# Queries of the first two token tiles from raw x with a ones column, and their normalised tiles transposed by DMA

## The chip, the cores and the metric

One core of one Trainium2 chip. The metric is the device time of one execution in microseconds; lower is better. Medians over several executions are quoted with their range. A ratio is the mean time of one kernel's fast runs over the mean of the other's fast runs of the same rounds, so it is not quite the ratio of the two medians.

A profile is one execution.

## The reference

Two layers, each made of a sliding local attention (32 heads of 32, 8 positions back at a distance of 2) and a dense block of 1024 to 3584 with GELU. Cut to what matters:

```python
x = A_x                                        # [1, 2048, 1024] bf16
for layer in range(2):
    n = layernorm(x)                           # no gain, no bias
    q, k, v = split(n @ wqkv)                  # [1024, 3072]
    logits = sum(q[s] * k[s - 2*w] for each of 8 w) * 32**-0.5
    x = x + (softmax(logits) * v windows) @ wo
    x = x + (gelu(layernorm(x) @ w1 + b1) @ w2 + b2)
```

## The kernel before

Tokens are worked in four groups of 512, each of four tiles of 128 tokens. The order for group 0 is: queries of tiles 0 and 1 (the weights arrive meanwhile), queries of tiles 2 and 3, then K and V of all four tiles, then queries and K of group 1 while VectorE does group 0's attention, and at about 123 us the output projection of group 0, which reads the attention output `oT`. All loads go out from one engine (SP) in program order, in one queue. Normalised tiles of group 1 and 2 reach their transposed form by transposing DMAs in that same queue.

The start, which the change replaces:

```python
load_x(0, 0, 2)                                 # tiles 0, 1
for k in range(0, KD, 2):                       # query weights in four pieces of 512 KB
    load_wq_piece(wq_first[k // 4], k)
    if k < 4: load_x(0, 2 + k // 2, 3 + k // 2)
...
warm_up(14)                                     # dummy matmuls, no result used
stats(0); stats(1)                              # VectorE, root on ScalarE
xn0 = norm(0); xn1 = norm(1, (0, 2 * P, D))
transpose_on_pe(xn0, ...); transpose_on_pe(xn1, ...)
stats(2); stats(3)
...
# then the queries of tiles 0 and 1 from the normalised, transposed tiles
```

```python
wk = load_qkv(1)                                # 2 x 1 MB
load_x(2)                                       # tiles 8 to 11
early_tiles = ln_early((1, None), (2, qk_next))
for _ in range(NTT): next(early_tiles)          # tiles 4..7: statistics, norm, DMA transpose
wv = load_qkv(2)                                # V weights, 2 x 1 MB, BEHIND the transposes
for _ in early_tiles: pass                      # tiles 8, 9
```

## Time and profile before

| | before |
|---|---|
| median of the first three runs | 1230.72 us (1230.47 to 1231.24) |
| first useful matmul | 8.26 us |
| K of group 0 starts on PE | 23.19 us |
| VectorE's first attention product | 26.82 us |
| second half of the V weights issued, landed | 27.09, 35.92 us |
| the same needed by PE | 37.86 us |
| last attention output of group 0 ready, needed | 123.92, 124.85 us |
| span of the profile | 1228.4 us |

The other shows itself as a place with nothing in it; this is PE's timeline around the start of V in the kernel before (start, length, instruction):

```profile
35.71 5.56 PE L117 MATMUL acc<-xnT,wt 128*128 128x512 bf16 x25
```

Twenty-five matmuls in one run, no bracket: the V weights were 37.86 - 35.92 = 1.94 us early, and no view of waits shows a margin. It has to be looked up from the landing of the transfer.

### The profile page before, as it was taken

Reading aid. Unit: us, or ns where it says so; the run is one execution under the profiler, and the core shown is the slowest. Engines: PE = TensorE matmul, PEld = TensorE weight load, DVE = VectorE, ACT = ScalarE, POOL = GpSimd, SP = SyncE. Lnnn points to the kernel's source line nnn. Section 1 sums busy time; section 2 is a strip of 40 time slices with the busy share of each in tenths; the row PEclk is TensorE's granted clock in tenths of the full one; section 3 lists DMA queues with packets and bytes.
Section 4 is the critical chain, followed back from the end, with each engine's and each line's share of the span. In section 5 each row is a group of like instructions: output and inputs, shape, how many; then the busy total and the mean of one; then the engine's idle time right before and its main releaser. Section 6 shows DMA issues by size and latency. Waiting matters only on the chain.

```text
span 1228.4 us, 13955 instructions
## 1 busy us (share of the span) xinstructions
PE 1221.6 (99%) x5720; PEld 632.7 (52%) x5770; DVE 861.5 (70%) x912; ACT 315.6 (26%) x497; POOL 120.9 (10%) x219
## 2 busy tenths in 40 slices
PE   9999999999999999999999999999999999999998
PEld 7666544456444564446544465444654444444444
DVE  7999896998898999375993759937599797011001
ACT  5343253014310233202431024410244001300310
POOL 2330025010101101100001000000000002000000
PEclk9999999999999999999999999999999999999999
DMA  9965674766638645856557565576664558446441
GB/s 302 290 206 164 176 233 151 202 178 199 219 128 245 188 150 166 239 170 175 161 158 230 172 171 181 157 216 201 171 200 147 186 194 209 149 159 194 156 135 52
DMA packets 223647, 226.64 MB, mean 185 GB/s; under 512 B 71824, under 2 KB 190752, under 8 KB 221536
## 3 DMA queue, kind: packets, MB, share of 16 engines
q1 hardware_dynamic: 214704, 208.69, 56.3%
q0 software_dynamic: 8880, 17.07, 4.2%
q8 instruction: 45, 0.74, 0.2%
q14 instruction: 18, 0.15, 0.0%
HBM read 189.01 MB, written 4.19 MB: 157 GB/s over the span
## 4 chain that ended last, share of the span: by engine, by line
PE 99%; DVE 0%; issue 0%; DMA 0%
PE acc L117 99%; DMA x<-in_A_x_dram 0%; DVE stats L92 0%; PE acc L211 0%; DVE xn L92 0%; DVE x L92 0%; DVE mv L92 0%; DVE rstd L92 0%
## 5 line engine op out<-in xcount | busy, mean ns | idle before, releaser
L117 PE MATMUL acc<-xnT,wt 128*128 128x512 bf16 (+1 forms) x3392 | 720.3, 375 | 0.1
L117 PEld LDWEIGHTS <-wt 128*128 128x128 bf16 x3392 | 400.8, 120 | 317.4
L117 PE MATMUL acc<-wt,hT 128*128 128x512 bf16 (+1 forms) x1780 | 386.0, 376 | 2.1
L117 PEld LDWEIGHTS <-hT 128*128 128x128 bf16 x1820 | 178.1, 98 | 209.0
L92 DVE TENSOR_TENSOR big<-big 128x1024 bf16<-128x1024 bf16 (+2 forms) x184 | 244.8, 1359 | 2.2
L92 ACT ACTIVATE hT<-acc,b1T 128x512 bf16<-128x512 f32 x224 | 152.1, 687 | 325.9 <-PE acc L117 325.8
L92 DVE TENSOR_TENSOR big<-qT,kT 128x4096 bf16<-128x4096 bf16 x64 | 143.8, 2283 | 36.3 <-ACT kT L92 35.9
L92 DVE TENSOR_TENSOR big<-abc,vT 128x4096 bf16<-128x4096 bf16 x64 | 144.6, 2284 | 11.0 <-DMA abc<-a 7.1
L92 DVE TENSOR_TENSOR tmp<-acc,b2bc 128x512 f32<-128x512 f32 x56 | 38.6, 689 | 159.8 <-PE acc L117 156.7
L92 ACT CAST qT<-acc 128x512 bf16<-128x512 f32 (+1 forms) x72 | 38.0, 543 | 276.8 <-PE acc L117 274.6
L117 PE MATMUL acc<-wt,oT 128*128 128x512 bf16 x440 | 97.6, 379 | 0.4
L92 DVE BATCH_NORM_STATS2 stats<-x 128x6 f32<-128x512 bf16 x116 | 77.4, 681 | 6.0 <-DMA x<-in_A_x_dram 5.0
L117 PEld LDWEIGHTS <-oT 128*128 128x128 bf16 x448 | 43.8, 98 | 53.0 <-issue 0.3
L92 DVE TENSOR_TENSOR x<-acc,big 128x512 bf16<-128x512 f32 (+1 forms) x9 | 5.7, 632 | 90.0 <-PE acc L117 90.0
L92 POOL TENSOR_TENSOR rstd<-mv,eps_t 128x1 f32<-128x1 f32 x54 | 16.7, 308 | 524.2 <-DVE mv L92 524.2
L92 ACT CAST vT<-acc 128x512 bf16<-128x512 f32 x64 | 37.4, 585 | 101.9 <-PE acc L117 101.9
L92 ACT CAST kT<-acc 128x512 bf16<-128x512 f32 x64 | 37.3, 584 | 64.5 <-PE acc L117 64.5
L92 DVE TENSOR_TENSOR x<-acc,x 128x512 bf16<-128x512 f32 x64 | 42.9, 670 | 5.1 <-PE acc L117 4.7
L92 DVE TENSOR_SCALAR xn<-x,mv,rstd 128x1024 bf16<-128x1024 bf16 (+2 forms) x53 | 28.5, 540 | 20.1 <-POOL rstd L92 19.9
L92 DVE TENSOR_TENSOR x<-tmp,x 128x512 bf16<-128x512 f32 x56 | 38.6, 689 | 1.4
L92 POOL DMA_DIRECT2D big<-big x24 | 13.3, 563 | 212.5 <-DVE big L92 212.5
L92 ACT ACT_TABLE_LOAD x17 | 21.8, 1283 | 38.9 <-DVE e L92 30.5
(62 smaller groups left out, 285.4 us busy)
## 6 DMA issues: line engine op xcount, KB each, us to landing
wt<-in_B_w_dram SPq DMA_DIRECT2D x56, 1024.0 KB, 5.6
wt<-in_B_w_dram SPq DMA_DIRECT2D x64, 896.0 KB, 4.8
wt<-in_A_wqkv_dram SPq DMA_DIRECT2D x46, 1024.0 KB, 5.6
wt<-in_A_wo_dram SPq DMA_DIRECT2D x16, 1024.0 KB, 5.0
abc<-a POOLq DMA_DIRECT2D x32, 256.0 KB, 4.6
big<-big POOLq DMA_DIRECT2D x24, 256.0 KB, 3.8
x<-in_A_x_dram SPq DMA_DIRECT2D x16, 256.0 KB, 7.1
out_dram<-x SPq DMA_DIRECT2D x31, 128.0 KB, 1.8
```

Source lines behind the costliest of these rows:

```text
L92: inst = f(*args, **kwargs)
L117: return pe(nc.tensor.matmul(*args, **kwargs))
```

## The change

The intent is to begin useful matmuls without waiting for VectorE's statistics. Layer normalisation is (x - mean) * rstd, so q = (x W - mean * sum(W)) * rstd. PE transposes the raw x of tiles 0 and 1, multiplies weights by it, and a column of ones beside the tokens (two are written, one is read) gives sum(W) in the same matmuls. Afterwards VectorE adds -mean * sum(W), and GpSimd multiplies by rstd. Mean and rstd lie by token on partitions and are needed along the free axis; four fp32 transposes on PE spread them. K and V still need the normalised tiles 0 and 1, which two DMA transposes now provide. The first loads are issued by two engines. Cut to its core:

```diff
-    load_x(0, 0, 2)
-    for k in range(0, KD, 2): load_wq_piece(...)         # 512 KB pieces, SP
+    SP:  x0, wq rows 0, 2, 3, x3, wq rows 5, 6, 7         # 256 KB pieces
+    ACT: x1, wq row 1, x2, wq row 4
...
-    warm_up(14)
-    stats(0); stats(1); norms; transposes of the normalised tiles
+    warm_up(8); transposes of raw x[0], x[1]; warm_up(4)
+    stats(0); root(0); stats(1); root(1)
+    less = -mean; rstd = 1 / root
+    norm(0), norm(1)                    -> first_early   (for K and V)
+    # after three of eight weight rows:
+    for column in (less0, less1, rstd0, rstd1):
+        pe(nc.tensor.transpose(bank[...], column.to_broadcast([P, P]), identf[:]))   # fp32
+    rest():  stats(2), root(2), norm(2), stats(3), root(3), norm(3)
...
+    def finish(c):
+        vec.scalar_tensor_tensor(out=part[:, c, :], in0=less, scalar=first[c][:, NT:NT + 1],
+                                 in1=first[c][:, 0:NT], op0=ALU.mult, op1=ALU.add)
+        pool.tensor_tensor(out=qT[:, c, 0:NT], in0=part[:, c, :], in1=rstd, op=ALU.mult)
+    for c in range(7): finish(c)        # ahead of the statistics of tile 4
...
-            wk = load_qkv(1)
+            for xn, out in first_early: sp.dma_start_transpose(out, xn...)
+            wk = load_qkv(1, lambda: load_x(1, 2, 3))     # tile 6 between the halves
+            load_x(1, 3, 4)                               # tile 7 behind them
...
-            ahead = ln_stats(tiles[i + 1][0])              # rstd by GpSimd
+            ahead = ln_stats(tiles[i + 1][0], root=True)   # root on ScalarE
+            vec.reciprocal(mv_rstd[1][:], mv_rstd[1][:])   # one more op on VectorE
```

More of the change, by code (lines that the diff above doesn't have):

```diff
@@ L119, with load_x, load_qkv @@
     x = [xpool.tile([P, D], BF16, name=f"x{t}") for t in range(S // P)]
-    def load_x(g, t0=0, t1=NTT):
+    def load_x(g, t0=0, t1=NTT, engine=None):
         for tt in range(t0, t1):
             t = g * NTT + tt
-            sp.dma_start(x[t][:], x_in[t * P:(t + 1) * P, :])
-    def load_qkv(which):
+            (engine or sp).dma_start(x[t][:], x_in[t * P:(t + 1) * P, :])
+    def load_qkv(which, between=None):
         tiles = []
@@ L130, in load_qkv, with load_wq_row @@
             sp.dma_start(wt[:], wqkv_v[:, h * (KD // 2):(h + 1) * (KD // 2), which * D:(which + 1) * D])
+            if h == 0 and between:
+                between()
             tiles.append(wt)
         return tiles
-    def load_wq_piece(wt, k):
-        sp.dma_start(wt[:, k % (KD // 2):k % (KD // 2) + 2, :], wqkv_v[:, k:k + 2, 0:D])
-    load_x(0, 0, 2)
+    def load_wq_row(k, engine):
+        engine.dma_start(wq_first[k // (KD // 2)][:, k % (KD // 2), :], wqkv_v[:, k, 0:D])
+    load_x(0, 0, 1)
     wq_first = [wpool.tile([P, KD // 2, D], BF16, name="wt") for _ in range(2)]
-    for k in range(0, KD, 2):
-        load_wq_piece(wq_first[k // (KD // 2)], k)
-        if k < 4:
-            load_x(0, 2 + k // 2, 3 + k // 2)
+    for k in (0, 2, 3):
+        load_wq_row(k, sp)
+    load_x(0, 3, 4)
+    for k in range(5, KD):
+        load_wq_row(k, sp)
     warm = bigp.tile([P, P], BF16, name="big")
@@ L150 @@
     one = const.tile([P, 1], F32, name="one")
+    act.on = True
     act.activation(one[:], eps_t[:], ACT.Sqrt)
+    load_x(0, 1, 2, act)
+    load_wq_row(1, act)
+    load_x(0, 2, 3, act)
+    load_wq_row(4, act)
+    act.on = False
     ident = const.tile([P, P], BF16, name="ident")
     make_identity(nc, ident[:])
+    identf = const.tile([P, P], F32, name="identf")
+    make_identity(nc, identf[:])
     mask = const.tile([P, W - 1, HALO], F32, name="mask")
@@ L174, in load_b2, with ln_stats @@
         pool.dma_start(b2bc[:], B_b2.unsqueeze(0).to_broadcast([P, D]))
-    def ln_stats(t, mv=None, rstd=None):
+    def ln_stats(t, mv=None, rstd=None, root=False):
         stats = lnp.tile([P, 2, 6], F32, name="stats")
@@ L183, in ln_stats @@
         vec.bn_aggr(mv[:], stats[:])
+        if root:
+            std = lnp.tile([P, 1], F32, name="std")
+            act.activation(std[:], mv[:, 1:2], ACT.Sqrt, bias=eps_t[:])
+            return mv, std
         pool.tensor_tensor(out=rstd[:], in0=mv[:, 1:2], in1=eps_t[:], op=ALU.add)
@@ L206, in ln_norm, with transpose_on_pe, copy_transposed @@
         return xn
-    def transpose_on_pe(xn, out, parts):
-        pst = psum.tile([P, KD, P], BF16, name="acc", bufs=8)
-        for k in range(parts[0][0], parts[-1][1]):
+    def transpose_on_pe(xn, out, bank, parts=(0, KD)):
+        pst = bank[:].bitcast(BF16).rearrange("p (k t) -> p k t", t=P)
+        for k in range(KD):
             pe(nc.tensor.transpose(pst[:, k, :], xn[:, k * P:(k + 1) * P], ident[:]))
-        for k0, k1, copy in parts:
-            copy(out[:, k0:k1, :], pst[:, k0:k1, :])
+        copy_transposed(out, bank, parts)
+    def copy_transposed(out, bank, parts):
+        pst = bank[:].bitcast(BF16).rearrange("p (k t) -> p k t", t=P)
+        for k0, k1 in zip(parts[:-1], parts[1:]):
+            act.copy(out[:, k0:k1, :], pst[:, k0:k1, :])
     last_transpose = [None]
@@ L220, in ln_tile @@
         last_transpose[0] = sp.dma_start_transpose(xnT[:, tt, :, :], xn[:].rearrange("s (k p) -> s k p", p=P))
-    first_late = []
+    first_early, first_late = [], []
+    NT = 2 * P
     def ln_first():
-        xa[0] = new_xnT()
+        xnT = xa[0] = new_xnT()
         vec.on = act.on = True
-        mvs = {}
-        stds = {}
+        raw = attp.tile([P, KD, NT + 2], BF16, name="vT", bufs=2)
+        vec.memset(raw[:, :, NT:NT + 2], 1.0)
+        mv = lnp.tile([P, 4, 2], F32, name="mvs", bufs=1)
+        std = lnp.tile([P, 4], F32, name="stds", bufs=1)
+        rstd = lnp.tile([P, 4], F32, name="rstds", bufs=1)
+        less = lnp.tile([P, 2], F32, name="lesses", bufs=1)
         def stats(tt):
@@ L234, in stats @@
                 vec.bn_stats(st6[:, h, :], x[tt][:, h * HALF:(h + 1) * HALF])
-            mvs[tt] = lnp.tile([P, 2], F32, name="mv")
-            vec.bn_aggr(mvs[tt][:], st6[:])
-            stds[tt] = lnp.tile([P, 1], F32, name="std")
-            act.activation(stds[tt][:], mvs[tt][:, 1:2], ACT.Sqrt, bias=eps_t[:])
-        def norm(tt, bounds=(0, D)):
-            rstd = lnp.tile([P, 1], F32, name="rstd")
-            vec.reciprocal(rstd[:], stds[tt][:])
-            xn = lnp.tile([P, D], BF16, name="xn", bufs=3)
-            for lo, hi in zip(bounds[:-1], bounds[1:]):
-                vec.tensor_scalar(out=xn[:, lo:hi], in0=x[tt][:, lo:hi], scalar1=mvs[tt][:, 0:1], scalar2=rstd[:],
-                                  op0=ALU.subtract, op1=ALU.mult)
-            return xn
+            vec.bn_aggr(mv[:, tt, :], st6[:])
@@ new lines, in root, with norm @@
+        def root(tt):
+            act.activation(std[:, tt:tt + 1], mv[:, tt, 1:2], ACT.Sqrt, bias=eps_t[:])
+        def norm(tt, out):
+            if tt > 1:
+                vec.reciprocal(rstd[:, tt:tt + 1], std[:, tt:tt + 1])
+            vec.tensor_scalar(out=out, in0=x[tt][:], scalar1=mv[:, tt, 0:1], scalar2=rstd[:, tt:tt + 1],
+                              op0=ALU.subtract, op1=ALU.mult)
+            return out
+        warm_ps = acc_tile()
+        warm_up(8, warm_ps)
+        banks = [acc_tile(), acc_tile()]
@@ L249, in ln_first @@
+        for tt in range(2):
+            transpose_on_pe(x[tt], raw[:, :, tt * P:(tt + 1) * P], banks[tt], (0, 2))
+        warm_up(4, warm_ps)
         stats(0)
+        root(0)
+        for tt in range(2):
+            copy_transposed(raw[:, :, tt * P:(tt + 1) * P], banks[tt], (2, KD))
         stats(1)
-        xn0 = norm(0)
-        xn1 = norm(1, (0, 2 * P, D))
-        transpose_on_pe(xn0, xa[0][:, 0, :, :], [(0, 2, act.copy), (2, 8, act.copy)])
-        transpose_on_pe(xn1, xa[0][:, 1, :, :], [(0, 2, vec.tensor_copy)])
@@ L255, in ln_first, with spread_stats @@
-        transpose_on_pe(xn1, xa[0][:, 1, :, :], [(2, 8, act.copy)])
-        stats(2)
-        stats(3)
-        for tt in range(2, 4):
-            first_late.append((norm(tt), xa[0][:, tt, :, :]))
-        vec.on = act.on = False
-        act.hold()
+        root(1)
+        vec.tensor_scalar(out=less[:], in0=mv[:, 0:2, 0], scalar1=-1.0, scalar2=None, op0=ALU.mult)
+        vec.reciprocal(rstd[:, 0:2], std[:, 0:2])
+        by_token = iop.tile([P, 4, P], F32, name="tmp")
+        def spread_stats(bank):
+            for i, column in enumerate((less[:, 0:1], less[:, 1:2], rstd[:, 0:1], rstd[:, 1:2])):
+                pe(nc.tensor.transpose(bank[:, i * P:(i + 1) * P], column.to_broadcast([P, P]), identf[:]))
+            rows = by_token[:].rearrange("p i t -> p (i t)")
+            act.copy(rows, bank[:])
+            return rows[:, 0:NT], rows[:, NT:2 * NT]
@@ new lines, in ln_first, with rest, queries_of_raw, row @@
+        xn = bigp.tile([P, 2, D], BF16, name="big")
+        first_early.append((norm(0, xn[:, 0, :]), xnT[:, 0, :, :]))
+        first_early.append((norm(1, xn[:, 1, :]), xnT[:, 1, :, :]))
+        def rest():
+            for tt in range(2, 4):
+                stats(tt)
+                root(tt)
+                xn = lnp.tile([P, D], BF16, name="xn", bufs=3)
+                norm(tt, xn[:])
+                first_late.append((xn, xnT[:, tt, :, :]))
+        return raw, spread_stats, rest
+    def queries_of_raw(wq, qT):
+        raw, spread_stats, rest = st.pop("raw")
+        first = {}
+        def row(c, k):
+            if k == 0:
+                first[c] = acc_tile()
+            mm(first[c][:, 0:NT + 2], lhsT=wq[k // (KD // 2)][:, k % (KD // 2), c::NCH], rhs=raw[:, k, :],
+               start=(k == 0), stop=(k == KD - 1), skip_group_check=True)
+        part = attp.tile([P, NCH, NT], F32, name="abc")
+        def finish(c):
+            vec.scalar_tensor_tensor(out=part[:, c, :], in0=less, scalar=first[c][:, NT:NT + 1], in1=first[c][:, 0:NT],
+                                     op0=ALU.mult, op1=ALU.add)
+            pool.tensor_tensor(out=qT[:, c, 0:NT], in0=part[:, c, :], in1=rstd, op=ALU.mult)
+        for k in range(KD):
+            for c in range(7):
+                row(c, k)
+                if (k, c) == (0, 6):
+                    bank = acc_tile()
+                if (k, c) == (2, 6):
+                    less, rstd = spread_stats(bank)
+                    rest()
+                if (k, c) in ((5, 3), (7, 3)):
+                    transpose_on_pe(*first_late.pop(0), bank)
+        act.on = False
+        act.hold()
+        for c in range(7):
+            finish(c)
+        for k in range(KD):
+            row(7, k)
+        vec.on = False
+        return lambda: finish(7)
@@ L308, in gen_qkv @@
         wq = wq_first if n == 0 else load_qkv(0)
-        if not v_first:
+        if n == 0:
+            for xn, out in first_early:
+                sp.dma_start_transpose(out, xn.rearrange("s (k p) -> s k p", p=P))
+            wk = load_qkv(1, lambda: load_x(1, 2, 3))
+            load_x(1, 3, 4)
+        elif not v_first:
             wk = load_qkv(1)
@@ L328, in gen_qkv @@
             wk = load_qkv(1)
+        qT = qk_pool.tile([P, NCH, T], BF16, name="qT")
         if n == 0:
+            last = queries_of_raw(wq, qT)
+            sp.on = True
             load_x(2)
             early_tiles = ln_early((1, None), (2, qk_next))
-            for _ in range(NTT):
+            for tt in range(NTT):
                 next(early_tiles)
+                if tt == 0:
+                    last()
             wv = load_qkv(2)
@@ L336, in gen_qkv @@
                 pass
+            vec.hold()
             load_x(3)
-        qT = qk_pool.tile([P, NCH, T], BF16, name="qT")
-        first = {}
-        for kq in range(4 if n == 0 else 0):
-            for c in range(7):
-                first[c] = qkv_chunk(wq, c, xnT, first.get(c), kq * (KD // 4), (kq + 1) * (KD // 4), 0, 2)
-                if (kq, c) == (2, 3):
-                    transpose_on_pe(*first_late.pop(0), [(0, KD, act.copy)])
-                if (kq, c) == (3, 4):
-                    for done in range(2):
-                        act.copy(qT[:, done, 0:2 * P], first[done][:, 0:2 * P])
-                    transpose_on_pe(*first_late.pop(0), [(0, KD, act.copy)])
-                    act.hold()
-        if n == 0:
-            first[7] = qkv_chunk(wq, 7, xnT, t0=0, t1=2)
-        for c in list(first)[2:]:
-            act.copy(qT[:, c, 0:2 * P], first[c][:, 0:2 * P])
+            sp.on = False
+            sp.hold()
         kT = qk_pool.tile([P, NCH, HALO + T], BF16, name="kT")
@@ L549, in gen_ffn2, with warm_up @@
                     yield
-    def warm_up(count):
-        ps = acc_tile()
+    def warm_up(count, ps):
         for _ in range(count):
@@ L568, in ln_early @@
         vec.on = True
-        ahead = ln_stats(tiles[0][0])
+        ahead = ln_stats(tiles[0][0], root=True)
         on_act = tiles[-2:]
@@ L615 @@
     pool.on = True
-    warm_up(14)
-    ln_first()
+    st["raw"] = ln_first()
     first = build_constants()
     with tc.tile_pool(name="early", bufs=1) as early:
-        load_x(1)
+        sp.on = True
+        load_x(1, 0, 2)
         stage(gen_qkv(0, qk_next=early), sides=at(9, ln_stats_ahead, 2, NTT - 2) + at(14, pool.dma_start, mask[0::NTT, :, :], first[:]) + at(11, ln_end) + at(14, load_b2))
```

## The prediction

> **What bounds the kernel now.** I read the chain of waits first. In the page it is one line of engines:
>
> ```profile
> PE 99%; DVE 0%; issue 0%; DMA 0%
> ```
>
> The span is the tensor engine's queue of matmuls, and only what delays or shortens that queue counts. So the next view is the same chain in order of time for the first 16 us, because the change works only there. Columns: start in us, length in us, what the chain ran through.
>
> ```profile
> 0.74 2.69 DMA x<-in_A_x_dram
> ...
> 4.99 1.16 DVE stats L92 x2
> ...
> 6.44 0.55 DVE xn L92
> ...
> 7.10 0.74 DVE xn L92 x2
> ...
> 7.89 0.51 PE acc L211 x6
> 8.40 4.01 PE acc L117 x36
> ```
>
> The first token tile arrives at 3.43, VectorE makes statistics of two tiles and normalises them, PE transposes, and then weights are multiplied without a break. PE's own timeline says what it does meanwhile:
>
> ```profile
> 0.99 6.02 PE L117 MATMUL acc<-big 128*128 128x512 bf16 x14 [0.99 <-DVE big L92]
> 7.05 1.35 PE L211 MATMUL acc<-ident,xn 128*128 128x128 bf16 x16
> 8.26 4.15 PE L117 MATMUL acc<-xnT,wt 128*128 128x256 bf16 x36
> ```
>
> Fourteen dummy matmuls fill 6.02 us, then 16 transposes, and the first matmul that counts starts at **8.26 us**. From there PE has no gap over 0.1 us up to 134 us. The prize is a part of these 8.26 us, 0.7% of the span.
>
> Now who could take it back. VectorE's timeline, columns start, length, instruction, and in brackets an idle time and its releaser:
>
> ```profile
> 13.31 1.29 DVE L92 BATCH_NORM_STATS2 stats<-x 128x6 f32<-128x512 bf16 x2 [0.58 <-DMA x<-in_A_x_dram]
> ...
> 21.85 1.29 DVE L92 BATCH_NORM_STATS2 stats<-x 128x6 f32<-128x512 bf16 x2 [1.50 <-DMA x<-in_A_x_dram]
> ...
> 26.35 0.55 DVE L92 TENSOR_SCALAR qT<-x,mv,rstd 128x1024 bf16<-128x1024 bf16 x1 [0.71 <-POOL rstd L92]
> 26.82 2.28 DVE L92 TENSOR_TENSOR big<-qT,kT 128x4096 bf16<-128x4096 bf16 x1
> ```
>
> From 26.82 us VectorE works on attention of the first group. Asked for its waits from 26.9 to 124 us, the profile gives one line:
>
> ```profile
> DVE big L92 <- DMA abc<-a: 1.9, 1, 1.9
> ```
>
> That is one fixed wait for a spread of the weights that VectorE itself made. Otherwise it is full for 97 us, and what it makes last is needed by PE at once:
>
> ```profile
> 123.17 0.75 DVE L92 TENSOR_TENSOR oT<-big 128x512 bf16<-128x512 bf16 x2
> ...
> 123.34 3.99 PE L117 MATMUL acc<-wt,oT 128*128 128x512 bf16 x16
> ```
>
> The last attention output is done at 123.92. PE takes the eighth slice of oT in its eighth matmul. A matmul of 512 columns takes 10.79/50 = 0.216 us (the chain prints 49 in 10.74, and a 0.05 issue), so it is due at 123.34 + 7 x 0.216 = 124.85. **VectorE has only about 0.9 us of slack there.**
>
> **What the Trainium skill says.** "TensorE: Matmul & The Clock Gate", Part 1: PE runs at half rate until a window of about 3.4 us has been busy, and the window is free-running; Part 4 adds that transposes do not count as busy in the same way. The trace agrees on the first: the 14 dummies are 6.02/14 = 0.43 us apart, twice the later 0.216. On the second no run here speaks. "DMA: Bandwidth & Descriptors", Issuing engines are not separate DMA queues: transfers from several engines share 16 DMA engines, and issuing from two only saves issue time. In the trace an issue takes 0.43 us, a 256 KB tile lands every 0.67 us while the queue is full, so issue is not the limit. "FP8 and Floating Point Precision", TensorE Precision Notes: true fp32 takes four passes. This trace has no fp32 matmul. "Advanced Engine Details and Errata", X-Bar Transpose (TRN2): transposing DMAs are about as fast as plain ones. The trace disagrees somewhat: the four transposes of 256 KB landed at 24.82, 25.75, 27.01 and 28.26, so 0.9 to 1.25 us each against 0.67.
>
> **The change part by part.**
>
> Start of PE. The instruction order of the new kernel on PE is 8 dummies, 16 transposes of raw x, 4 dummies, then weights against raw x. The dummies end at 0.99 + 8 x 0.43 = 4.4. The second tile, now issued by ScalarE in parallel with the first, should land near the 4.25 of before. Transposes at half rate take 16 x 0.107 = 1.7, so 6.1. Four dummies take 1.7 us cold or 0.9 warm: 7.0 to 7.8. Before, the rate was full by 7.05; I take 7.3 for the first useful matmul, **1.0 us earlier**. The weights hardly allow more: before, the first two weight rows landed at 7.22, the fourth unit of 256 KB in a queue that gives one every 0.67. Statistics are no longer before the first matmul, which is the intent.
>
> Work added on PE: 64 matmuls of 258 instead of 256 columns, 64 x 2/2.4 ns, nearly nothing. Four fp32 transposes: if four passes at a bf16 transpose's 0.056 us, 4 x 4 x 0.056 = 0.9 us (estimate; 0.2 if one pass). I take 0.5. So PE is 0.5 us ahead when the first seven query chunks are finished, near 14.9.
>
> Work added on VectorE: eight corrections that read PSUM. Before, an add of 128x256 from PSUM took 0.42 alone; in a row I take 0.35. Seven of these stand ahead of the fourth tile's statistics, that is 2.5 us; they cannot end before the seven chunks do, at about 15.5 to 16.5. Those statistics began at 13.31 before. Then come six tiles as before, at about 1.85 us each (16.57 to 18.41), each with one more reciprocal of 0.15, and one more correction; the 1.5 us wait and 0.7 us wait for GpSimd may go. From 13.31 to 26.9 there were 13.6 us, less 2.2 of waits, plus 6 x 0.15 + 0.37 + 0.3 for the square roots on ScalarE: 13.0. Started at 15.9, the end is 28.9, **2.0 us later**.
>
> DMA: two transposes of 256 KB now stand in the queue ahead of the K weights and tiles 6 to 9, which were full-queue bound until 22.5 us. At 0.9 to 1.2 each, tile 8 lands 1.8 to 2.4 us after its 21.83. From there to 26.9 the old chain took 5.07; the new one has some 0.2 less. This too says 1.6 to 2.2 us later. Both paths agree on about **2 us of delay for VectorE's first attention product**.
>
> Sum. That delay runs through 97 us of full VectorE to the last oT: 123.92 + 2.0 = 125.9, against a need at 124.85 - 0.5 = 124.35. PE waits about 1.55 us there and has gained 0.5: **net +1.0 us**. The gain at the start drops out: the end of this stage is VectorE's, and the time is before + (delay - 0.9), whatever PE won. 1230.7 + 1.1 = 1231.8. After that stage VectorE waits for PE again, so I expect the shift to be carried unchanged to the end.
>
> **The rivals.**
>
> A, PE keeps its gain. If VectorE is delayed by under 0.4 us (corrections overlap waits that were there anyway, two issuing engines fill the slow first 6 us of DMA better), the gain of 0.5 to 1.0 stands: 1229.8 to 1230.3. For it: 2.2 us of VectorE waits exist to be used. Against it: full DMA queue, and in-order VectorE.
>
> B, the cold clock. If transposes of raw x do not count as busy, PE may stay at half rate until near 10 us, and real matmuls pay: some 20 at 0.215 instead of 0.109, up to 2 us, which eats the start's gain and delays the corrections too. About 1232 to 1233. For it: only 8 dummies run in a row, under 3.5 us. Against: the window hardly empties.
>
> C, K weights late. The second half of these landed at 21.15, K began at 23.19. Two transposes and one x tile move it to about 22.5 to 23, and its use is 0.86 us after K's start: a short stall is possible, but it only takes from the wait at oT. Time as in the sum.
>
> **Range and chances.** 2% is 24 us, three times the whole start; nothing here reaches it. Faster 0.01, within 2% 0.98, slower 0.01. For the time I take 1231.7, between the sum and rival A. The low end 1229.9 is rival A, the high end 1233.1 is the sum with 3 us of VectorE delay, or B.
>
> **What would show it.** First matmul on wt and raw x near 7.3 (step one); fp32 transposes 0.2 to 0.9 us in sum; VectorE's first big<-qT,kT near 28.8 instead of 26.82 (the decisive step); a PE gap of about 1.5 us at the first oT matmuls near 123 to 126, released by VectorE. Wrong if there is no such gap, if the first product starts before 27.3, or if matmuls after the start come at 0.215 us.

## The result

| | before | after | after, second profile |
|---|---|---|---|
| median | 1230.32 us (1229.98 to 1231.24, 6 runs) | 1231.34 us (1231.11 to 1232.13, 6 runs) | 1231.52 us (1230.87 to 1232.21, 5 runs) |
| ratio to before, 95% | | 1.0009 (0.9996 to 1.0022) | 1.0010 (0.9996 to 1.0023) |
| first useful matmul | 8.26 | 6.32 | 5.92 |
| K starts | 23.19 | 22.99 | 22.60 |
| first attention product | 26.82 | 29.53 | 29.66 |
| V weights, second half landed | 35.92 | 39.00 | 36.82 |
| last `oT` ready | 123.92 | 125.42 | 125.57 |
| PE waits after K's start | none listed | 1.2 us, V weights | 1.0 us, `oT` |
| span | 1228.4 | 1229.5 | 1229.1 |

The kernel comes out about 1 us later by the medians; a difference of zero is still inside the interval. The second profile belongs to a later job, in which before had 1230.38 us (1230.09 to 1231.10, 9 runs).

**The start.** PE's timeline after the change, first profile:

```profile
1.00 3.60 PE L117 MATMUL acc<-big 128*128 128x512 bf16 x8 [1.00 <-DVE vT L92]
4.38 1.23 PE L226 MATMUL acc<-ident,x 128*128 128x128 bf16 x16
5.45 1.03 PE L117 MATMUL acc<-big 128*128 128x512 bf16 x4
6.32 2.57 PE L117 MATMUL acc<-vT,wt 128*128 128x258 bf16 x21
8.72 0.38 PE L289 MATMUL acc<-identf,lesses 128*128 128x128 f32 x2
8.94 0.38 PE L289 MATMUL acc<-identf,rstds 128*128 128x128 f32 x2
9.16 2.15 PE L117 MATMUL acc<-vT,wt 128*128 128x258 bf16 x18
11.64 0.62 PE L226 MATMUL acc<-ident,xn 128*128 128x128 bf16 x8 [0.33 <-DVE xn L92]
...
14.29 0.61 PE L226 MATMUL acc<-ident,xn 128*128 128x128 bf16 x8 [0.48 <-ACT xnT L92]
```

Weights meet raw x 8.26 - 6.32 = 1.94 us earlier than weights met normalised x. Then read the starts, not the lengths: the fp32 transposes occupy 8.72 to 9.16, 0.44 us for four. Two brackets are new. At 11.64 PE wants the normalised tile 2 and VectorE has just made it; at 14.29 it wants the bank in which tile 2 was transposed, and ScalarE frees it late, because the root for tile 3 stands ahead of that copy in its program. Counted as the lengthening of the step, the two cost 0.49 and 0.65 us. So 1.94 - 0.44 - 1.14 = 0.36 us should be left when K starts; it is 0.21 us, and for the other 0.15 I have no cause.

**VectorE.** Its timeline after the change, first profile, at the corrections, the first product and the last output:

```profile
14.04 2.85 DVE L92 SCALAR_TENSOR_TENSOR abc<-tmp,acc 128x256 f32<-128x256 f32 x7
16.81 1.28 DVE L92 BATCH_NORM_STATS2 stats<-x 128x6 f32<-128x512 bf16 x2
...
22.73 1.29 DVE L92 BATCH_NORM_STATS2 stats<-x 128x6 f32<-128x512 bf16 x2
...
29.53 2.28 DVE L92 TENSOR_TENSOR big<-qT,kT 128x4096 bf16<-128x4096 bf16 x1
```

Seven corrections take 2.85 us. Statistics of tile 4 start at 16.81 where they started at 13.31. Those at 22.73 are tile 7's, and tile 7 landed at 22.71, behind the two DMA transposes: VectorE arrives there just as the tile does, so two causes of the same size stand behind the delay. The first product is 2.71 us late.

**Where PE waits.** The list of PE's waits, the chain of waits near V, and PE's timeline there, first profile:

```profile
PE acc L117 <- DMA wt<-in_A_wqkv_dram: 1.2, 1, 1.2
```

```profile
28.89 10.11 DMA wt<-in_A_wqkv_dram
```

```profile
35.72 2.11 PE L117 MATMUL acc<-xnT,wt 128*128 128x512 bf16 x9
39.05 2.16 PE L117 MATMUL acc<-xnT,wt 128*128 128x512 bf16 x9 [1.22 <-DMA wt<-in_A_wqkv_dram]
```

The run of 25 matmuls of before is cut in two: the load of the V weights was issued at 28.89, 1.80 us later than before, took 10.11, and PE stood. By the length of that step (1.22 is what the list counts) it lost 1.39 us, which is all that the time from K's start to the end grew by. There is no wait at `oT`. In the second profile of the same kernel it is the other way round; the list of waits and PE's and VectorE's timelines near the output projection are:

```profile
PE acc L117 <- DVE oT L92: 1.0, 1, 1.0
```

```profile
122.75 1.53 PE L117 MATMUL acc<-wt,oT 128*128 128x512 bf16 x5
125.29 2.88 PE L117 MATMUL acc<-wt,oT 128*128 128x512 bf16 x12 [1.02 <-DVE oT L92]
```

```profile
124.82 0.75 DVE L92 TENSOR_TENSOR oT<-big 128x512 bf16<-128x512 bf16 x2
```

Here V landed at 36.82, in time, and PE reached the output projection undelayed and waited for VectorE there. From K's start to the end of the program both profiles take 1206.5 us, against 1205.2 before. In this pair, whichever of the two deadlines came first took the wait, and the other then cost nothing more.

What moved the V weights by 2 us between two executions of one kernel? The throughput of the DMA engines from 24 to 39.5 us, in slices of 0.39 us, first profile and then second:

```profile
GB/s 333 215 65 214 294 181 8 106 282 291 290 255 158 0 0 6 10 173 354 344 333 402 370 349 418 365 402 396 365 423 349 418 298 244 26 21 26 17 210 282
```

```profile
GB/s 351 272 98 154 281 291 289 87 8 184 241 319 229 4 7 9 203 372 344 418 365 402 391 370 412 365 407 359 402 391 370 309 293 279 293 288 130 307 333 254
```

Both halt from 29.0 us on, the first until 30.6 and the second until 30.2, while transposing DMAs of group 1 are in flight. The first halts again at 37.2 to 38.7, with those of group 2 in flight, and the last few packets of the V weights are caught in it.

### The profile page after: what moved, and what is told of

The parts are those of the page before. It is cut to its first block, busy times and chain, and to the rows that moved or that the text cites. A ratio compares the mean times of both kernels' runs of the same rounds, so it can differ in the third digit from the quotient of the medians.

```text
span 1229.5 us, 13979 instructions
## 1 busy us (share of the span) xinstructions
PE 1220.8 (99%) x5722; PEld 632.6 (51%) x5772; DVE 865.4 (70%) x925; ACT 315.4 (26%) x497; POOL 121.5 (10%) x217
## 4 chain that ended last, share of the span: by engine, by line
PE 98%; DMA 1%; DVE 0%; ACT 0%; issue 0%
PE acc L117 98%; DMA wt<-in_A_wqkv_dram 1%; DVE stats L92 0%; ACT vT L92 0%; PE acc L226 0%; DVE big L92 0%; ACT stds L92 0%; ACT xnT L92 0%; DVE xn L92 0%; DVE mvs L92 0%; DVE x L92 0%; DVE rstds L92 0%; DVE vT L92 0%
## 5 line engine op out<-in xcount | busy, mean ns | idle before, releaser
L92 ACT CAST qT<-acc 128x512 bf16<-128x512 f32 (+1 forms) x64 | 35.5, 558 | 279.4 <-PE acc L117 276.2
L92 DVE TENSOR_SCALAR xn<-x,mv,rstd 128x1024 bf16<-128x1024 bf16 x48 | 26.2, 545 | 19.7 <-POOL rstd L92 19.7
```

Of the source, the lines that this page charges most:

```text
L92: inst = f(*args, **kwargs)
```

## The experiments

All were timed in five rounds; before had medians of 1230.19, 1230.58, 1230.38 and 1230.30 us (9 runs each) in the four jobs. The table has each kernel's one profile. "K to end" is the span less the start of K, good to 0.1 us: what the start won or lost is not in it. One thing of the start remains: a late K gives every deadline behind it more room. "Product - K" is how far VectorE's first attention product is behind K's start. The second half of the V weights is needed 14.67 us after K starts, in the fifth matmul of V's first chunk.

| run | median us (range) | ratio (95%) | K starts | product - K | V landed - K | PE waits after K (us) | K to end |
|---|---|---|---|---|---|---|---|
| before | see above | | 23.19 | 3.63 | 12.72 | none | 1205.2 |
| after | 1231.34 | 1.0009 | 22.99 | 6.54 | 16.02 | V 1.2 | 1206.5 |
| again (after) | 1231.52 | 1.0010 | 22.60 | 7.06 | 14.22 | oT 1.0 | 1206.5 |
| v_early | 1231.29 (1230.79 to 1231.81) | 1.0010 (0.9997 to 1.0022) | 22.91 | 6.84 | 15.33 | V and group 1, 1.3 in all | 1207.1 |
| no_corr | 1231.66 (1231.43 to 1231.82) | 1.0012 (1.0000 to 1.0025) | 24.57 | 5.15 | 13.22 | none | 1205.2 |
| no_dmat | 1231.99 (1231.30 to 1232.59) | 1.0014 (1.0002 to 1.0027) | 23.46 | 6.51 | 15.85 | V 1.1 | 1206.8 |
| one_queue | 1232.19 (1231.72 to 1233.43) | 1.0018 (1.0004 to 1.0031) | 23.40 | 6.91 | 16.39 | V 1.6 | 1207.0 |
| both | 1230.66 (1229.99 to 1230.79) | 0.9999 (0.9986 to 1.0011) | 23.67 | 4.72 | 12.88 | none | 1205.2 |
| thin | 1231.43 (1230.88 to 1231.89) | 1.0006 (0.9993 to 1.0018) | 22.99 | 6.75 | 14.20 | oT 0.4, group 1 0.2 | 1206.2 |
| thin67 | 1231.96 (1230.78 to 1233.12) | 1.0012 (0.9998 to 1.0025) | 23.01 | 5.77 | 15.62 | V 0.8, group 1 0.8 | 1207.2 |
| x67 | 1231.86 (1230.93 to 1234.26) | 1.0015 (1.0002 to 1.0027) | 23.65 | 6.51 | 16.08 | V, group 1, 3.0 in all | 1208.9 |
| s2 | 1232.51 (1231.90 to 1233.41) | 1.0017 (1.0005 to 1.0030) | 23.33 | 6.01 | 15.79 | V 1.0, group 1 0.6 | 1207.4 |
| s3 | 1232.76 (1232.18 to 1233.68) | 1.0020 (1.0007 to 1.0032) | 22.88 | 7.19 | 15.92 | weights 2.3 in 4 places, 0.3 at one more | 1209.0 |
| c2 | 1233.75 (1233.58 to 1235.27) | 1.0028 (1.0014 to 1.0042) | 22.76 | 4.59 | 11.39 | group 1 2.6 | 1209.6 |

The waits are those that the list of waits names. It undercounts: "K to end" grew by 0.1 to 0.7 us more than the list in most runs, by 1.3 in s3 and by 1.9 in c2. c2's profile had a granted clock of 0.998, all others 1.0.

### v_early: the V weights earlier in the queue

```diff
-            for tt in range(NTT):
-                next(early_tiles)
-                if tt == 0: last()
-            wv = load_qkv(2)
+            wv = load_qkv(2, group_one)      # first half, then tiles 4..7, then second half
```

> The first half of the V weights is issued ahead of the four DMA transposes of group 1, nothing else changes. Theory Q (the loss is one PE wait of 1.39 us for V weights, issued late because they stand on SP behind transposes that wait for VectorE): the second half lands before 37.6 instead of 39.0, the wait at V goes. VectorE still ends the last oT near 125.4, and PE would need it at 124.7, so a wait of about 0.7 appears at the first oT matmuls: time 0.6 us under the changed kernel, about 1230.7. Theory Q' (V weights are the only loss, nothing behind it): 1.3 us under, about 1230.0, no wait at oT. Theory P (as predicted: VectorE's last oT is the bound already): unchanged, 1231.3.

A right kernel. The first half landed at 28.48, the second only at 38.24, because four transposes, landing until 33.66, now stood between them. By the length of the steps PE waited 0.7 us at V and 0.9 us more at 59.98 us, for weights of group 1, which landed at 59.93. Nothing was won. The second half came later than theory Q allowed (37.6), and theory P's time came true without its wait at `oT`. I read it so: the queue is busy between 24 and 60 us, a transfer put ahead pushes others back, and the wait moved down the queue.

### no_corr: no corrections

```diff
-            vec.scalar_tensor_tensor(...); pool.tensor_tensor(...)
+            act.copy(qT[:, c, 0:NT], first[c][:, 0:NT])
```

> The eight corrections of the raw queries (VectorE, then GpSimd) are replaced by eight ScalarE copies of 128x256, as before the change; the result is wrong on purpose. Theory C (the corrections, 2.85 us on VectorE ahead of tile 4's statistics, make VectorE, then the transposes, then the V weights late): VectorE's first product starts near 27.0 instead of 29.5, V weights land before 37.6, no PE wait at V, last oT near 123.5 to 124; time about 1230.1, 1.2 under the changed kernel. Theory D (two added DMA transposes in the queue make everything late): first product after 28.5, V still after 38.5, time within 0.4 of 1231.3.

Its output is wrong, which doesn't matter for the time. The first product still came at 29.72 us: with VectorE free earlier, it waited 1.26 us for tile 7 instead (and 1.14 us for a root on ScalarE, which now made the copies). So the corrections alone are not what makes VectorE late. PE has no wait behind K, but K itself started 1.6 us later than in the change, partly from the clock (below), partly because ScalarE's copies held a bank (a PE wait of 0.8 us at 16.69). The experiment therefore says nothing on what the time would be without corrections; its reading is VectorE's wait.

### no_dmat: no DMA transposes of tiles 0 and 1

```diff
-                sp.dma_start_transpose(out, xn.rearrange("s (k p) -> s k p", p=P))
+                pool.memset(out, 0.0)
```

> The two DMA transposes of tiles 0 and 1 are replaced by GpSimd memsets of the same tiles; the result is wrong on purpose. Theory C: VectorE is not waiting for data from tile 4 on, so its first product stays at 29.3 to 29.6, V lands after 38.3, time within 0.4 us of 1231.3. Theory D: tiles 6 to 9 land 2 us earlier, first product near 28, V before 37.6, time about 1230.0.

Its output is wrong, which doesn't matter for the time. Tile 7 landed at 20.9 instead of 22.71, so the two transposes took 1.8 us of the queue. Yet the first product came at 29.97 and V landed at 39.31: VectorE was now held by the corrections. The transposes alone are not the cause either.

### one_queue: all first loads from one engine

```diff
-    SP: x0, w0, w2, w3, x3, w5, w6, w7    ACT: x1, w1, x2, w4
+    SP: x0, x1, w0, w1, w2, x2, w3, x3, w4, w5, w6, w7
```

> All first loads are issued by SP in the order in which they landed in the changed kernel (x0 x1 w0 w1 w2 x2 w3 x3 w4 w5 w6 w7), none by ScalarE. If a second issuing engine only saves issue time (0.45 us each, x1 0.3 later, w4 1 us), landings stay within 0.5 us: w0 5.3 to 5.8, w7 before 12; first useful matmul 6.3 to 6.8. If two queues fill the DMA engines better in the first 6 us, one queue lands w0 near 6.6 and w7 near 12.6 as before the change, and the first useful matmul comes at 6.8 to 7.3. The time moves by under 0.7 us, as later waits are set by VectorE and DMA.

A right kernel, 1.0018 to before; the change has 1.0009, and the two intervals overlap. The first twelve pieces had all landed at 12.19 us instead of 11.40, and from the fourth piece on each was 0.3 to 0.8 us later. In all twelve profiles with two issuing engines the twelfth landed between 11.15 and 11.63, so they do bring something in the first microseconds. The wait at V stayed.

### both, thin, x67: the two causes alone and together

`thin` keeps VectorE's place in the pipeline but makes a correction a copy of two columns:

```diff
-            vec.scalar_tensor_tensor(out=part[:, c, :], ...)
-            pool.tensor_tensor(out=qT[:, c, 0:NT], ...)
+            vec.tensor_copy(qT[:, c, 0:2], first[c][:, 0:2])
+            pool.memset(qT[:, c, 2:NT], 0.0)
```

`x67` loads tiles 6 and 7 earlier, with everything else kept:

```diff
+            load_x(1, 2, 4)
             for xn, out in first_early: sp.dma_start_transpose(...)
-            wk = load_qkv(1, lambda: load_x(1, 2, 3))
-            load_x(1, 3, 4)
+            wk = load_qkv(1)
```

`both` is `thin` with the memset of no_dmat.

> Both suspected causes of VectorE's lateness are taken out at once (wrong result on purpose): the seven corrections shrink to copies of two columns, and the two new DMA transposes become a memset on GpSimd. Theory P (VectorE is late for two overlapping reasons, the corrections and tile 7 that lands behind the transposes, each able to hold it alone; late VectorE holds the transposes of group 1, these hold the V weights in the load queue): the first attention product starts at 27 to 28 instead of 29.5, the second half of the V weights lands before 37.4, PE has no wait for it and none at the attention output near 124, and the time is set by the start alone: span 1228.2 + (start of K - 23.19), so with K at 22.9 to 23.9 a time of 1229.8 to 1230.8. Rival R (the load queue is late by itself, by instruction fetch and queue order, whatever VectorE does): V weights land at 38.5 or later and PE waits 0.7 to 1.4 us as in the change.

> The corrections alone shrink to copies of two columns on VectorE (wrong on purpose); the two DMA transposes stay. Theory P: VectorE is free at 15 but now waits for tile 7, which lands at about 22.7; the first product comes at 28.6 to 29.7 and the V weights still make PE wait 0.3 to 1.4 us. If corrections were the only cause, the first product comes before 28 and there is no wait at V.

> A right kernel: tiles 6 and 7 are loaded ahead of the two new DMA transposes and of the K weights. Theory P: tile 7 lands near 14 to 15, yet VectorE stays bound by the corrections: first product at 28.5 to 29.7, V weights land between 38 and 39.3, PE waits 0.3 to 1.4 us for them. If the tile's late landing were the only cause, the first product comes before 28 and the wait at V goes. Rival C: the second half of the K weights lands later by some 0.7 us, near 22.7, and PE waits for it by a few tenths at 23.8.

In `both` the first product comes at 28.39, a little later than the 27 to 28 expected, and the rest is as expected: V lands at 36.55, the list of PE's waits is empty behind 17 us, and K to end is 1205.2 us, that of before. PE's timeline of `both` at V, and VectorE's first products:

```profile
35.76 3.62 PE L117 MATMUL acc<-xnT,wt 128*128 128x512 bf16 x16
```

```profile
28.39 6.69 DVE L92 TENSOR_TENSOR big<-qT,kT 128x4096 bf16<-128x4096 bf16 x3
```

The extra wait for V is thus put down to these two additions: without them V lands 1.8 us before it is needed. It is one profile, but V lands 12.88 us behind K in it, and 14.22 and 16.02 in the two of the change. For `oT` the profile is less clear, because K started late and gave it room. The last `oT` came at 124.92. Before the change it was due 124.85 - 23.19 = 101.66 us after K; here that is 125.33, but with K at 22.99, as in the change, it would be 124.65, and about 0.3 us of wait might remain (my estimate, if VectorE kept its times).

That `both` is still no faster than before has two reasons. In its profile the full clock came late (6.84 us), the first useful matmul was at 7.33, and K started at 23.67. And K comes 16.34 us after the first useful matmul, against 14.93 before: with the earliest start seen, 5.92, it would have started at 22.26, 0.9 us ahead (an estimate).

`thin` alone: product at 29.74, held by tile 7 (VectorE waits 1.9 us for tiles 6 and 7). It missed in one point: V landed at 37.19, in time, and PE then waited 0.4 us at `oT`. `x67` alone: product at 30.16, held by the corrections; V landed at 39.73, and PE waited 3.0 us in all. These are outside its ranges, but its profile is of the slowest of its five runs (1234.26, median 1231.86). Each cause alone keeps VectorE's product 6.5 to 6.8 us behind K in these two and in `no_dmat`; in `no_corr` it is at 29.72 too, behind a later K.

### thin67: VectorE relieved, the DMA transposes kept

> The corrections shrink to two-column copies (wrong on purpose) and tiles 6 and 7 are loaded ahead of the two DMA transposes, which stay. It tells the late landing of tile 7 from the mere load of two more transposes on the queue. Theory P (VectorE's lateness counts, not the queue's load): the first attention product starts 4.4 to 5.3 us after K, the V weights land within 14.6 us of K's start, PE has no wait over 0.2 us at V or at the attention output, and from K's start to the end it is 1205.1 to 1205.6 us as before. Rival R (the load of two more transposes is what hurts): the product is early, and yet V lands 15 us or more after K's start and PE waits 0.5 us or more.

Its edit is that of `thin` and that of `x67` together. Its output is wrong, which doesn't matter for the time. Here my theory fell. VectorE was early, 5.77 us behind K (the expectation was 4.4 to 5.3; tile 8 now landed late, at 24.00), and PE did not wait at `oT`. But V landed 15.62 us behind K and PE waited for it, and again for group 1's weights:

```profile
PE acc L117 <- DMA wt<-in_A_wqkv_dram: 1.6, 2, 0.8
```

The rival's number, 15 us or more, came true in this profile. Its queue was full up to 26.9 us with tiles 8 to 11, the group-1 transposes landed one after the other behind them with one halt, at 27.78, 28.79, 31.25 and 32.02, and V followed. VectorE's work for these transposes was done by 26.2. So the V weights are late by the load of the queue too. How much of it is load and how much chance, one profile cannot tell: its five timed runs spread from 1230.78 to 1233.12, wider than before's 0.5 us.

Nor did the early product bring an early `oT`. The product was 0.75 us earlier than in the change, yet the last `oT` came at 125.76 instead of 125.42, because VectorE waited longer for the spread of the attention weights:

```profile
DVE big L92 <- DMA abc<-a: 1.7, 1, 1.7
```

From the product to the attention weights `a` VectorE takes 56.46 us in both, and from the end of that wait to the last `oT` 34.29; between them lie 6.23 us here and 5.15 in the change. PE had no wait at `oT` only because it was late itself: without its own waits it would have needed the last `oT` at 23.01 + 101.66 = 124.67.

### c2, s2, s3: right kernels that try to keep the gain

`c2` puts statistics of tiles 2 and 3 ahead of norms 0 and 1, loads tiles 6 and 7 first, puts the two DMA transposes between the halves of the K weights and both halves of the V weights ahead of three transposes of group 1, and moves a third tile's statistics to ScalarE. `s2` is `x67` with four of eight corrections moved off VectorE; `s3` has the same four moved, and the reordered statistics and the loads up to the K weights of `c2`:

```diff
+            if c >= 4:
+                act.copy(part[:, c, :], first[c][:, 0:NT + 2])
+                pool.tensor_scalar(out=corr, in0=less, scalar1=part[:, c, NT:NT + 1], op0=ALU.mult)
+                pool.tensor_tensor(out=corr, in0=corr, in1=part[:, c, 0:NT], op=ALU.add)
+                pool.tensor_tensor(out=qT[:, c, 0:NT], in0=corr, in1=rstd, op=ALU.mult)
```

> A right kernel that tries to keep the gain of the start. Statistics of tiles 2 and 3 come ahead of the normalised tiles 0 and 1; tiles 6 and 7 are loaded ahead of the K weights, and the two DMA transposes stand between the halves of these; both halves of the V weights stand ahead of three of group 1's transposes; the statistics of a third tile of group 2 go from VectorE to ScalarE, and that group's end one chunk earlier. Theory P: PE's two waits near 11.6 and 14.3 (0.5 and 0.65 us) lose at least 0.4 us together, V lands before 35, PE does not wait for it, the first product comes at 26.5 to 28.5, and what is left is a wait of up to 1 us for group 1's weights near 59 or at the attention output near 123. K starts at 21.8 to 23.2 and the time is 1229.0 to 1230.8. Rival R': the queue has no room at all between 24 and 60 us, and a new wait of 1 us or more takes the place of the one at V: 1231 or more.

> A right kernel: four of the eight corrections leave VectorE (ScalarE copies the sums out of PSUM, GpSimd does the product, the sum and the scaling), and tiles 6 and 7 are loaded ahead of the two new DMA transposes. Theory P: both causes of the late VectorE are cut by about as much as 1.7 us of work, so the first attention product starts at 27.7 to 28.7 instead of 29.5, the V weights land before 37.8, and PE waits at most 0.3 us for them and at most 0.4 us at the attention output; 1229.8 to 1231.0. Rival R (the queue is late by itself): V lands after 38.3 and the wait of 0.7 us or more stays.

> A right kernel: the same four corrections leave VectorE; statistics of tiles 2 and 3 come ahead of the normalised tiles 0 and 1; tiles 6 and 7 are loaded ahead of the K weights and the two DMA transposes stand between the halves of these. Theory P: K starts 15.7 to 16.0 us after the first useful matmul (16.68 in the change), so at 22.0 to 22.8; first attention product at 27.3 to 28.7; V weights land before 37.5. What PE may still wait for is up to 0.6 us at V, for group 1's weights or at the attention output. Time 1229.3 to 1230.6. Rival R: a wait of 0.8 us or more comes back at one of the three, 1230.8 or more.

All three missed and are slower than before with intervals that exclude 1. `c2` did what it should at first: K 15.87 us behind the first useful matmul instead of 16.68, product at 27.35, V at 34.15. Then VectorE lost what it had won in a wait of 3.65 us, and PE stood for group 1's weights (VectorE's and PE's timelines):

```profile
37.80 2.29 DVE L92 TENSOR_TENSOR big<-qT,kT 128x4096 bf16<-128x4096 bf16 x1 [3.65 <-ACT kT L92]
```

```profile
53.97 2.35 PE L117 MATMUL acc<-xnT,wt 128*128 128x512 bf16 x5 [2.56 <-DMA wt<-in_A_wqkv_dram]
```

The profile names ScalarE's K copy as releaser of the first wait, but the third K chunk, which this product reads, had been copied at 29.8 us. The product writes into the third of three buffers, which holds group 1's normalised tiles until their last transpose has landed, and that landed at 37.25, behind the V weights that I had put ahead of it. I take this to be the cause, from the times alone. PE's wait follows from the queue as well: the half of group 1's weights that it wanted landed at 53.9. It also cost more than its length: in this profile the clock was at half rate from 53.72 to 57.13, and the next matmuls came 0.427 us apart instead of 0.216, about 1.6 us more. Three of the five timed runs, the median among them, show a clock of 1.0, so this is not what makes `c2` slow in general.

In `s2` four corrections took VectorE 1.67 us instead of 2.85 for seven, but its later instructions became longer while GpSimd worked. The same normalisation of 128x1024, twice in a row:

```profile
27.55 1.23 DVE L92 TENSOR_SCALAR qT<-x,mv,std 128x1024 bf16<-128x1024 bf16 x1
28.70 0.14 DVE L92 RECIPROCAL std<-std 128x1 f32<-128x1 f32 x1
28.88 0.55 DVE L92 TENSOR_SCALAR qT<-x,mv,std 128x1024 bf16<-128x1024 bf16 x1
```

It takes 0.55 us alone and up to 1.23 in this stretch; with the others (0.73, 0.67, 0.65) this gives back 1.1 us, and the product came at 29.34. The Trainium skill, "SBUF — State Buffer", SBUF: two separate sides, says that GpSimd shares a port pair with those VectorE instructions that use two ports or read two inputs from SBUF, and that the one that comes second blocks for the other's whole instruction. That this normalisation is such an instruction is not shown; the trace agrees in kind, with 0.68 us added while a GpSimd instruction of 0.73 us ran from 27.63. Work moved to GpSimd was not free for VectorE. `s3`, with the same four moved, had its product at 30.07.

### again: the changed kernel once more

> The changed kernel once more, unaltered, for a comparison in the same job and a second profile. 1231.0 to 1231.9. Theory P: first useful matmul between 6.2 and 7.3 according to when the full clock comes, K 16.68 after it, first attention product 29.3 to 30.4, and a PE wait for the V weights of 0.7 to 1.7 us.

Reported above: 1231.52 us, and a PE wait at `oT` instead of at V. My theory expected a wait for V of 0.7 to 1.7 us and a first useful matmul at 6.2 or later (it came at 5.92), and both were misses. It is the most useful run: it shows that the V wait of the first profile was one of at least two outcomes.

## Why the prediction was right or wrong

**The time.** 1231.7 was predicted, 1231.34 measured, within the range, and the net of +1.0 us is what the medians show. (One end of the range is loose: by the prediction's own sum 3 us of delay give 1230.7 + 3 - 0.9 = 1232.8, not 1233.1.)

**Start of PE.** Predicted 7.3 for the first useful matmul; 6.32 and 5.92 came. The step was too careful, but not uniformly wrong: over twelve profiles with this start the value lies between 5.92 and 7.33, mostly according to when the full clock arrives (3.76 us in `v_early`, 6.84 in `both`). The free-running window of about 3.4 us in the Trainium skill, "TensorE: Matmul & The Clock Gate", Part 1, fits this spread of 3.1 us: the same eight dummies ran each time. Rival B (the clock stays cold until 10 us) did not occur; in the first profile the rate was full by 4.73.

**Gain at K.** Predicted 0.5 us of lead, measured 0.21 and 0.59. The reason was not the one given: the larger gain was taken back by two waits of 0.49 and 0.65 us that the prediction did not see. The fp32 transposes were put at 0.5 us and took 0.44.

**VectorE.** Predicted 2.0 us later, measured 2.71 and 2.84: the term was undersized by 0.7 to 0.8. The two paths given for it, corrections and the full queue, are both real: `no_corr`, `no_dmat`, `thin` and `x67` show that each alone keeps the product at 29.7 to 30.2, and removing both brings it to 28.39 (`both`) or 28.78 (`thin67`). The second path named the wrong tile, though. It counted from tile 8, which landed at 23.38, 1.55 us later than before, and VectorE reached that only at 24.78; tile 7, at 22.71, is the one that it met. The seven corrections were put at 2.5 us and took 2.85.

**The fixed wait.** The prediction called the 1.9 us wait for `abc` fixed. It was not: after the change VectorE waits only 0.6 us there, so 1.3 us of its delay was absorbed. It was the spread that took less time: VectorE could go on 6.43 us after `a` before the change, 5.15 and 5.16 after it, 5.78 in `both` and 6.23 in `thin67`. What sets this was not tested. By luck it offsets the undersized term: the last `oT` came at 125.42 and 125.57, where 125.9 had been predicted. VectorE's list of waits between 26.9 and 124 us after the change:

```profile
DVE big L92 <- DMA abc<-a: 0.6, 1, 0.6
```

**The wait at oT.** In the second profile the mechanism is as predicted, only smaller: 125.57 - 123.92 = 1.65 us of delay, less 0.93 of slack, is 0.72 us; the span grew by 0.7. In the first profile the step "PE waits about 1.55 us there" fails: there is no wait at `oT`, since PE had already stood 1.2 us at V. The failed step is that the sum knew one deadline behind K. There are at least three, and the second was the load queue's: V weights 1.94 us ahead of need before the change, behind two more transposes after it. The third is the half of group 1's weights for which PE waits in `v_early` and `thin67`. It is needed about 35.4 us after K (by `thin`, where it landed at 58.66 and held PE for 0.3 us). Before the change it landed at 57.24, 1.3 us early; after it, at 59.61, which would have been late had PE not stood at V. Rival C looked at the right queue, but at the K weights, which did not make PE wait.

That the time came out right in spite of this is in part luck. With PE already delayed at V, the delay at `oT` is covered and not added. But the size in the first profile is V's, 39.00 - 35.92 - 1.94 = 1.14 us; the path that the prediction had would have given 125.42 - 123.92 - 0.93 = 0.57.

**What stays open.** Why the DMA engines halt while transposing DMAs are in flight, for 0.8 us before the change (34.9 to 35.6) and up to 1.6 after it, is not shown. An instruction fetch of 16 KB is served just before or in the halt at 29 us (in the first profile at 29.00, for 0.94 us, while a 256-byte packet took 1.97 us); the Trainium skill, "Runtime: NRT & Kernel Launch", Instruction fetch mechanics, calls the cost of such a fetch mostly hidden. That fetches cause the halts was not tested, and no fetch lies near the halt at 37.2 us that held up the V weights: the only two between 23 and 41 us of that profile are at 25.71 and 29.00. Nor is it settled how much of V's lateness is queue load and how much is these halts: two profiles of one kernel differ by 2.2 us.

## What to carry to other kernels

An early gain reaches the end only if every deadline behind it has slack: list them all, the engine that feeds PE and the transfers that stand behind its work in the queue, with the margin of each, since a margin shows in no list of waits. A test run that stands at one deadline says nothing about the next: its wait there may be hidden. When two deadlines are of the same size, the wait can change place from one execution to the next while the total stays; profile such a kernel twice before naming a cause. And test two suspected causes singly and together: here neither removal alone helped VectorE, and both together did.

## What the Trainium skill lacked or had wrong

- "FP8 and Floating Point Precision", TensorE Precision Notes, gives four passes for true fp32 and does not name transposes; "TensorE: Matmul & The Clock Gate", Terms, mentions a transpose mode of trn2 that is four times faster for fp32. No page that I read gives a duration. The four fp32 transposes of 128x128 started 0.109 us apart, about twice a bf16 transpose at full clock (16 in 0.89 us, 0.056 each).
- "DMA: Bandwidth & Descriptors", Issuing engines are not separate DMA queues, says that a second issuing engine saves only issue time, and that this is usually small. It could say that at a start it is not: with two, the first twelve pieces of 256 KB had landed at 11.15 to 11.63 us (twelve profiles), with one at 12.19 (one profile).
- "Advanced Engine Details and Errata", X-Bar Transpose (TRN2), calls transposing DMAs as fast as plain ones. Here the first two delayed what was behind them by 1.8 us together, about 0.9 each, against 0.67 us for a plain tile of the same 256 KB. This is against that section only: a table in "DMA: Bandwidth & Descriptors" has a lower rate for some layouts. Transposes in flight also went together with halts of the DMA engines of 0.8 to 1.6 us (slices of 0 to 26 GB/s), of which no page that I read speaks.
- "TensorE: Matmul & The Clock Gate", Part 1, lets the point of full clock vary by 500 ns either way. The same start reached it at 3.76 to 6.84 us in different profiles, and the first useful matmul moved from 5.92 to 7.33 us. The page's other remark, that the count of slow matmuls varies from run to run, agrees.
